# Linear attention and a top-2 mixture of experts in one kernel: the gates of both token groups in one pass behind the second list, the loads of the attention tiles and of the last weight parts moved, small work moved out of the attention loop

## The chip, the cores and the metric

The kernel runs on one core of a Trainium2 chip. The metric is the device time of one run in microseconds (us), taken as the median of several runs.

## The reference

Everything is float32. First comes a linear attention with decay, for 4 batches, 8 heads, 768 steps and a head width of 48. Its output, 3072 tokens of 384 numbers, goes into a mixture of 8 experts of which each token takes two.

```python
for t in range(S):                       # S = 768, per batch and head
    cur = einsum('bhd,bhe->bhde', u[None] * kt, vt)
    y[:, :, t] = einsum('bhd,bhde->bhe', rt, state + cur)
    state = w[None, :, :, None] * state + einsum('bhd,bhe->bhde', kt, vt)
x = y.transpose(0, 2, 1, 3).reshape(3072, 384)
logits = x @ w_gate
noisy = logits + log1p(exp(x @ w_noise)) * noise
top2 = argpartition(-noisy, 2, axis=1)[:, :2]
top2_l = take(noisy, top2) - max
top2_w = exp(top2_l); top2_w /= top2_w.sum(-1) + 1e-9
for e in range(8):                       # w1[e]: 384 x 1024, w2[e]: 1024 x 384
    out[mask] += top2_w[mask] * (maximum(x[mask] @ w1[e], 0) @ w2[e])
```

## The kernel before

**The attention loop** runs over 24 tiles of 128 tokens, `for i in range(NT)`, six chunks of each of four batches. The states of tile `i` come from chunk to chunk, so a batch's next chunk follows four tiles later. For a tile, GpSimd makes the decayed keys `kd` (`prep_k`, L402, two tiles ahead of use) and the product for the `u` term `rku` (L410 and L414, or L421 late in the loop). TensorE turns them (L225), forms the scores `PAB` (L476), the state products `RV` (L494) and the output `py` (L531). VectorE scales `rT` (L464), masks the scores into `am` (L484), updates the state (`z`, L504 and L507), reduces the `u` term to `c` (L444, in `uterm_b`), multiplies `cv` (L448, up to tile 8; later ScalarE does it), and writes the tile's tokens `x` (`xout`, L560). From tile 13 on (`PE8`) TensorE forms `c` with a product (L433), and `uterm_b` copies it (L442). `x` is turned and multiplied by both gate matrices for the logits.

**SyncE's queue** carries the loads of `k` and `r` (`load(i + 5, (0, 2))`), `v` (`load(i + 4, (2, 3))`), the noise (`load_nz`, in tiles 5 to 8), the stores of `x` into the DRAM buffer `xd`, and the parts of expert 0's weights. It works through them in the order in which they are written.

**Expert 0's weights** are loaded and split into high and low halves inside the loop, in seven parts: `W_LD` maps the tile to the part that is loaded at its end, `W_AT0` holds the tile from which a part is split. Parts 0 to 2 are w1 (`w0h`, `w0l`), parts 3 to 6 are w2 (`w1h`, `w1l`). ScalarE writes the high halves, VectorE the low halves of the parts 0 to 3 (L356 and L359, 128x512 or 128x384), GpSimd those of parts 4 to 6 (`W_POOL = 4`).

**Routing** is done in two groups of 12 tiles. `route(g)` is a generator of small VectorE steps that other work calls for (`rstep`, `steps`), with a few TensorE products: softplus, top 2, ranks by prefix sums, then for each list `drop`, which places token numbers with products by TensorE (`place`, L709). `route(0)` runs in tiles 13 to 23. Its last part, `gates`, is an exponential in 12 small steps on 128x12 (L591 to L605), then L842 to L847, then the gate columns `gd` (L851, L854), which SyncE stores beside the tokens in `xd`. At tile 22 the first list is ready: `rows` writes its token numbers (L883 to L885), and `xgather` fetches the first three token tiles with indirect DMAs of GpSimd (L1020).

```python
        while i == I_EARLY and not early_done:      # I_EARLY = 22
            rstep(1)
            maybe_early()
        if i == I_EARLY and (0, 0) not in XG:
            xgather(0, 0, 0)
```

**The experts** follow, 8 experts of two chunks each: `p1` (products `ph`, L1131), the relu on ScalarE and VectorE (L1135, L1137), and `p2` (products `pym`, L1167). The first `p1` starts right behind the last tile; `zero_out` clears the output meanwhile. `route(1)`, the second list (`list_0`), group 1's gates and their gathers (`gates_0`, `ggather`), the full lists (`rest`) and `list_1` run beside the first three chunks. Behind chunk `s == 2`, `tile_counts` (L987 to L1003) sets the counts by which later tiles are skipped. A flag that the decay `w` lies outside its allowed range is computed in the attention loop (`next(flag)` at tiles 4 and 6: L321 to L323 on VectorE, L326 on TensorE, L327 and L328 on VectorE); it and the counts decide whether a slow path runs at the end.

## Time and profile before

| | |
|---|---|
| median of 3 runs | 589.64 us (589.39 to 593.2) |
| profiled execution, its own time | 589.92 us |
| its span in the trace | 588.2 us |
| TensorE busy | 568.2 us, 97% |
| VectorE, ScalarE, GpSimd busy | 348.1, 284.5, 280.0 us |

The profiled execution took 1.7 us more than its span, since the run's time includes the start and the end around it. TensorE is busy for most of the span, so the share of busy time says little; what is of interest is the first quarter, where the attention loop, the handover to the experts and the routing lie.

### The profile page before, as it was taken

To read this page: it belongs to the slowest core of one execution; us is meant where nothing else is said; L and a number is where in the kernel's file an instruction comes from. 1 tells how busy PE (TensorE), PEld (TensorE's weight loads), DVE (VectorE), ACT (ScalarE), POOL (GpSimd) and SP (SyncE) were. 2 spreads that over 40 slices of the span, in tenths; PEclk is the share of its full clock that TensorE was granted. 3 is DMA by queue.
4 is the path that set the end of the run, shared out by engine and by line. 5 is a ranking of instruction groups with operands and counts; after the bars stand their busy time and mean duration, and the time that the engine had idled before them with its cause. 6 is when DMAs were issued, how large, how long until landed. Compare 5 with 4: busy or idle time off the path is not lost.

```text
span 588.2 us, 13907 instructions
## 1 busy us (share of the span) xinstructions
PE 568.2 (97%) x5383; PEld 543.4 (92%) x5384; DVE 348.1 (59%) x788; ACT 284.5 (48%) x712; POOL 280.0 (48%) x416
## 2 busy tenths in 40 slices
PE   8899899989999999999999999999999999999995
PEld 5799888879989999999999999999999999999995
DVE  7998698888864544556454554546363546454331
ACT  4348766842363624455445444454454455445220
POOL 8999455740336443436345453434262436423222
PEclk9999999989999999999999999999999999999999
DMA  8999889258405644765655646365845546424211
GB/s 166 224 219 205 201 202 210 83 142 258 125 35 189 184 131 120 189 138 175 108 154 164 177 116 200 98 184 127 173 118 153 169 127 187 124 82 85 67 35 42
DMA packets 143225, 86.53 MB, mean 147 GB/s; under 512 B 118624, under 2 KB 133215, under 8 KB 143152
## 3 DMA queue, kind: packets, MB, share of 16 engines
q1 hardware_dynamic: 132368, 56.76, 40.3%
q0 software_dynamic: 10160, 28.81, 16.0%
q8 instruction: 44, 0.72, 0.5%
q14 instruction: 29, 0.24, 0.1%
q10 hardware_dynamic: 624, 0.00, 0.1%
HBM read 58.81 MB, written 19.86 MB: 134 GB/s over the span
## 4 chain that ended last, share of the span: by engine, by line
PE 89%; DVE 5%; POOL 2%; issue 2%; ACT 1%; DMA 1%; POOLq 0%; ACTq 0%
PE ph L1131 37%; PE pym L1167 34%; PE py L531 4%; PE PAB L476 3%; PE pym L1160 2%; PE pym L1158 2%; PE KX L225 2%; PE py L569 1%; DVE am L484 1%; PE RV L494 1%; POOL kd L402 1%; PE RV L225 1%; PE RV L182 1%; PE RT L709 1%; PE ptm L1049 1%
## 5 line engine op out<-in xcount | busy, mean ns | idle before, releaser
L1167 PE MATMUL pym<-w1h,hb 128*128 128x384 f32 x768 | 200.3, 337 | 0.0
L1137 DVE SCALAR_TENSOR_TENSOR hb<-ph,hb 128x384 fp32r<-128x384 f32 x128 | 71.1, 556 | 116.7 <-ACT ht L1135 74.2
L1167 PEld LDWEIGHTS pym<-w1h,hb 128*128 128x128 f32 x768 | 139.3, 188 | 0.2
L1131 PE MATMUL ph<-xh,w0h 128*128 128x384 f32 (+1 forms) x384 | 136.0, 354 | 0.0
L1131 PE MATMUL ph<-xh,w0l 128*128 128x384 f32 (+1 forms) x384 | 135.6, 353 | 0.0
L1131 PE MATMUL ph<-xl,w0h 128*128 128x384 f32 (+1 forms) x384 | 130.4, 353 | 0.0
L1167 PE MATMUL pym<-w1l,hb 128*128 128x384 f32 x384 | 129.2, 336 | 0.0
L1135 ACT ACTIVATE hb<-ph 128x384 fp32r<-128x384 f32 x128 | 62.9, 492 | 106.7 <-PE ph L1131 106.7
L1192 POOL DMA_INDIRECT out_dram<-ot,TK x56 | 60.1, 1073 | 97.2 <-DVE ot L1186 42.1
L1020 POOL DMA_INDIRECT xg<-xd,GR x56 | 62.0, 1107 | 49.2 <-DVE r_e L603 24.4
L1131 PEld LDWEIGHTS ph<-xh,w0h 128*128 128x128 f32 x384 | 72.6, 189 | 3.5
L1131 PEld LDWEIGHTS ph<-xh,w0l 128*128 128x128 f32 x384 | 72.6, 189 | 3.1
L1131 PEld LDWEIGHTS ph<-xl,w0h 128*128 128x128 f32 x384 | 72.5, 189 | 3.2
L1035 POOL DMA_INDIRECT pv<-out_dram,GA x49 | 50.3, 1026 | 52.4 <-DMA out_dram<-ot,TK 39.7
L1167 PEld LDWEIGHTS pym<-w1l,hb 128*128 128x128 f32 x384 | 72.1, 188 | 0.1
L1105 ACT ACTIVATE xh<-xj 128x384 fp32r<-128x384 f32 (+1 forms) x42 | 21.1, 502 | 43.3 <-DVE xj L1103 43.1
L1175 ACT ACTIVATE ot<-pym 128x384 f32<-128x384 f32 x42 | 20.4, 486 | 39.9 <-PE pym L1167 33.1
L1106 DVE TENSOR_TENSOR xl<-xj,xh 128x384 fp32r<-128x384 f32 (+1 forms) x42 | 22.5, 535 | 24.8 <-ACT xh L1105 24.8
L1091 ACT ACTIVATE pl<-xg 128x768 uint16<-128x768 uint16 (+1 forms) x42 | 35.3, 841 | 1.4 <-DMA xd<-pl 1.4
L484 DVE TENSOR_TENSOR am<-PAB,mneg 128x512 int32<-128x512 int32 x48 | 30.8, 682 | 4.9 <-PE PAB L476 4.5
L476 PE MATMUL PAB<-rT,kT 64*128 64x128 f32 x384 | 27.7, 280 | 3.6 <-issue 3.2
L453 ACT ACTIVATE cv<-vt,c 128x48 f32<-128x48 f32 x120 | 30.2, 324 | 0.2
(276 smaller groups left out, 826.8 us busy)
## 6 DMA issues: line engine op xcount, KB each, us to landing
stg<-in_moe_w_dram SPq DMA_DIRECT2D x24, 512.0 KB, 4.7
stg<-in_moe_w_dram SPq DMA_DIRECT2D x32, 384.0 KB, 3.7
xd<-x SPq DMA_DIRECT2D x24, 196.0 KB, 3.3
rd<-in_r_dram SPq DMA_DIRECT2D x24, 192.0 KB, 4.3
vt<-in_v_dram SPq DMA_DIRECT2D x24, 192.0 KB, 4.3
out_dram<-ot SPq DMA_DIRECT2D x16, 288.0 KB, 4.1
kt<-in_k_dram SPq DMA_DIRECT2D x23, 192.0 KB, 3.8
xg<-xd,GR POOLq DMA_INDIRECT x56, 3.2
```

Source lines behind the costliest of these rows:

```text
L453: nc.scalar.activation(CV[i][:, h, :], vt[i][:, h, :], AF.Copy, scale=C8[i][:, h, :])
L476: nc.tensor.matmul(pa[:, s, p, :], kT[i][s * 64:(s + 1) * 64, p, :], rT[i][s * 64:(s + 1) * 64, p, :], start=True, stop=True)
L484: nc.vector.tensor_tensor(am[:, :, h].bitcast(I32), pa[:, :, h].bitcast(I32), mneg[:, None].to_broadcast([128, 2, NP // 2, 128]), op=ALU.b ...
L531: nc.tensor.matmul(o[qs], lhsT[:, qs], rhs, start=first[q], stop=last, skip_group_check=True)
L1020: nc.gpsimd.indirect_dma_start(out=xg[:n, :XW if e else DM], out_offset=None, in_=xd[:rows_of(early_)], in_offset=bass.IndirectOffsetOnAxi ...
L1035: nc.gpsimd.indirect_dma_start(out=pv[:n], out_offset=None, in_=out, in_offset=bass.IndirectOffsetOnAxis(ap=GA[:n, e * NJ + t:e * NJ + t + ...
L1091: nc.scalar.activation(pl[:n], XG[e, t][:n, :DM].bitcast(U16).rearrange("p (d two) -> p two d", two=2), AF.Copy)
L1131: nc.tensor.matmul(ph[:, :w_], a[:, d, fs], x[:, d, :w_], start=(j == 0), stop=(j == len(q) - 1))
L1135: nc.scalar.activation(h_[:, f, 0, :], ph[:, a:b], AF.Relu)
L1137: nc.vector.scalar_tensor_tensor(h_[:, f, 1, :], ph[:, a:b], 0.0, h_[:, f, 0, :].bitcast(F32), op0=ALU.max, op1=ALU.subtract)
L1167: nc.tensor.matmul(py, hb[:, f, a, hs], x[:, f, :], start=(j == 0), stop=(j == len(q) - 1))
L1192: st = nc.gpsimd.indirect_dma_start(out=out, out_offset=bass.IndirectOffsetOnAxis(ap=TK[:n, q:q + 1], axis=0), in_=ot[:n], in_offset=None, ...
```

## The change

It moves work, and removes little of it.

- **Loads.** From tile 8 on, `k` and `r` are loaded four tiles ahead and `v` three, in place of five and four; tile 8 itself loads nothing.
- **Weights.** Parts 4, 5 and 6 are loaded at tiles 15, 18 and 19 (before: 14, 16, 18) and split from tiles 18, 20 and 21 (before: 17, 19, 21). The low halves of parts 5 and 6 are VectorE's now.
- **Gates.** Both groups' gates are one pass, 24 wide, behind the second list. Group 0's exponential and gate store leave the loop; `route(1)` takes the first steps of group 0's full list (`rest_pre`) in their place.
- **First list.** `maybe_early` is called right behind `xout`, and the first token tile is fetched before GpSimd's `rku` of tile 23, the other two behind it.
- **Small work.** The two constants `ltri` and `ie_n` go to ScalarE at tile 5, the third into the slow path; the flag goes behind chunk `s == 2`; `uterm_b(i + 1)` runs behind `mask(i + 1)` in tiles 1 to 7 (it ran before `xout(i)`); a memset of GpSimd goes from tile 4 to tile 10; group 1's first `drop` places its products one step later (`lag` 3).

```diff
-W_LD = {3: 0, 5: 1, 7: 2, 9: 3, 14: 4, 16: 5, 18: 6}
-W_AT0 = (6, 8, 10, 12, 17, 19, 21)
-W_POOL = 4
+W_LD = {3: 0, 5: 1, 7: 2, 9: 3, 15: 4, 18: 5, 19: 6}
+W_AT0 = (6, 8, 10, 12, 18, 20, 21)
+AHEAD = (5, 4)
+I_FAR = 8
+W_POOL = (4,)
...
     def consts_v():
-        nc.vector.tensor_scalar(ltri, idif, 0.0, None, op0=ALU.is_gt)
-        nc.vector.tensor_copy(ieu, ie)
-        nc.vector.tensor_scalar(ie_n[:, 0, :], ie, float(LS), None, op0=ALU.mult)
+        nc.scalar.activation(ltri, mneg[:, 0, :], AF.Copy, scale=-1.0)
+        nc.scalar.activation(ie_n[:, 0, :], ie, AF.Copy, scale=float(LS))
...
-                              nc.gpsimd if len(units) >= W_POOL else nc.vector))
+                              nc.gpsimd if len(units) in W_POOL else nc.vector))
...
+    def rest_pre(g):
         i0, i1 = GROUPS[g]
         yield from slots(g)
         yield 0.2
-        for c in pairs(g, SLI[:, :, i0:i1], SL[g], "d"):
+        for PRE[g] in pairs(g, SLI[:, :, i0:i1], SL[g], "d"):
             yield 0.2
...
+    def gates(gs, lists=True):
+
+        i0, i1 = GROUPS[gs[0]][0], GROUPS[gs[-1]][1]
+        e2 = rtp[0].tile([128, NT], F32, name="r_e2", bufs=1)[:, :i1 - i0]
+        dn = GTS[:, 1, i0:i1]
+        yield from expneg(dn, [128, i1 - i0], "r2", e2)
+        nc.vector.tensor_scalar(dn, e2, 1.0, 1e-9, op0=ALU.add, op1=ALU.add)
+        yield
+        nc.vector.reciprocal(GTS[:, 0, i0:i1], dn)
+        yield
+        nc.vector.tensor_mul(dn, e2, GTS[:, 0, i0:i1])
+        yield
+        for g in gs if lists else ():
...
+            nc.sync.dma_start(xd[i0 * 128:i1 * 128, DM:].rearrange("(n p) e -> p n e", p=128), gd)
+            yield 0.25
...
         for _ in range(3):
-            next(ex, None)
+            next(behind, None)
+            next(behind, None)
             yield
...
-            yield from drop(g, *c, IJ_0, NJ, 0, g == 0)
+            yield from drop(g, *c, IJ_0, NJ, 0, g == 0, 3 if g else 2)
         routed.add(g)
-        if lists and not g:
-            while not early_done:
-                yield "wait"
-            for c in GATES[0]:
-                yield c
...
-        if early_done and (0, 0) not in XG:
-            xgather(0, 0, 0)
-        if i + 5 < NT:
-            load(i + 5, (0, 2))
-        if i in (4, 6):
-            next(flag)
+        if early_done and (0, 2) not in XG:
+            xgather(0, 0, 0, [t for t in chunks(0)[0] if (0, t) not in XG])
+        if i + AHEAD[i >= I_FAR] < NT and i != I_FAR:
+            load(i + AHEAD[i >= I_FAR], (0, 2))
...
-        if i == B:
+        if i == 10:
             consts_b()
...
-        if i + 4 < NT:
-            load(i + 4, (2, 3))
+        if i + AHEAD[i >= I_FAR] - 1 < NT and i != I_FAR:
+            load(i + AHEAD[i >= I_FAR] - 1, (2, 3))
...
-        if i and i + 1 < NT:
+        if CV_DVE <= i < NT - 1:
             uterm_b(i + 1)
         steps(1)
         xout(i)
...
-        if i == I_EARLY and (0, 0) not in XG:
-            xgather(0, 0, 0)
+        maybe_early()
+        if early_done and (0, 0) not in XG:
+            xgather(0, 0, 0, chunks(0)[0][:1 if i < I_EARLY else 3])
...
-                steps(3)
...
             mask(i + 1)
-            if not i:
+            if i < CV_DVE:
                 uterm_b(i + 1)
             steps(3)
             maybe_early()
-        if not i:
+        if i == 5:
             consts_v()
...
-            yield from GATES[1]
+            yield from gates((0, 1))
...
         if s == 2:
+            for _ in flag:
+                pass
             tile_counts(CAP)
```

The line numbers of the changed kernel are one higher than those of the kernel before for most of what follows. On **SyncE's queue around tile 8** before (`stg` is a weight part, `nz` the noise, `kt`, `rd` and `vt` the loads of k, r and v, of the tiles 13, 13, 12, 14, 14 and 13 in this order; the two `xd` stores are of the tiles 8 and 9):

```order
L348 DMA stg<-in_moe_w_dram 128x1024
L157 DMA kt<-in_k_dram 128x8x48
L157 DMA rd_103<-in_r_dram 128x8x48
L174 DMA nz<-in_moe_noise_dram 128x6x8
L157 DMA vt<-in_v_dram 128x8x48
L562 DMA xd<-x_146 128x392
L157 DMA kt<-in_k_dram 128x8x48
L157 DMA rd_104<-in_r_dram 128x8x48
L157 DMA vt<-in_v_dram 128x8x48
L562 DMA xd<-x_147 128x392
L348 DMA stg<-in_moe_w_dram 128x2x384
```

and the same place in the changed kernel, where the loads are of the tiles 13, 13, 12 and, in the last row, 14:

```order
L349 DMA stg<-in_moe_w_dram 128x1024
L176 DMA nz<-in_moe_noise_dram 128x6x8
L563 DMA xd<-x_146 128x392
L159 DMA kt<-in_k_dram 128x8x48
L159 DMA rd_103<-in_r_dram 128x8x48
L159 DMA vt<-in_v_dram 128x8x48
L563 DMA xd<-x_147 128x392
L349 DMA stg<-in_moe_w_dram 128x2x384
L159 DMA kt<-in_k_dram 128x8x48
```

The `xd` store of tile 8 and the noise stand ahead of the loads of tile 13 now; the store of tile 9 and the weight part stand ahead of the `k` load of tile 14.

On **VectorE from the end of tile 21 to the `x` of tile 23** (the last row of each) before; the twelve rows begin behind the list rows L883 to L885, which stand behind the `am` of tile 22 there, and the first `x` is of tile 22:

```order
L600 TENSOR_SCALAR r_e_2139<-r2r 128x12
L442 COPY c_2869<-py 128x8
L603 SCALAR_TENSOR_TENSOR r_e_2139<-r_e_2139,r2r 128x12
L560 TENSOR_TENSOR x_148<-py,cv 128x384
L603 SCALAR_TENSOR_TENSOR r_e_2139<-r_e_2139,r2r 128x12 x2
L484 TENSOR_TENSOR am<-PAB,mneg 128x2x256 x2
L603 SCALAR_TENSOR_TENSOR r_e_2139<-r_e_2139,r2r 128x12 x2
L605 SCALAR_TENSOR_TENSOR r_e_2139<-r_e_2139,r2s 128x12
L842 TENSOR_SCALAR GTS<-r_e_2139 128x12
L845 RECIPROCAL GTS<-GTS 128x12
L847 TENSOR_TENSOR GTS<-r_e_2139,GTS 128x12
L560 TENSOR_TENSOR x_149<-py,cv 128x384
```

and in the changed kernel, where the rows begin with those of the list, and `rT` and the first `am` are of tiles 23 and 22:

```order
L884 SCALAR_TENSOR_TENSOR lt<-L 128x3
L885 TENSOR_SCALAR lt<-lt 128x3
L886 TENSOR_SCALAR GR<-lt 128x3
L465 TENSOR_TENSOR rT<-RV,pwr 128x2x4x64
L485 TENSOR_TENSOR am<-PAB,mneg 128x2x256 x2
L357 TENSOR_TENSOR w1l_1322<-stg,w1h_1321 128x384
L443 COPY c_2848<-py 128x8
L561 TENSOR_TENSOR x_148<-py,cv 128x384
L485 TENSOR_TENSOR am<-PAB,mneg 128x2x256 x2
L360 TENSOR_TENSOR w1l_1322<-stg,w1h_1321 128x384
L357 TENSOR_TENSOR w1l_1322<-stg,w1h_1321 128x384
L561 TENSOR_TENSOR x_149<-py,cv 128x384
```

The list's three rows come ahead of `rT` of tile 23, the rows of the gates (L600 to L847) are gone from ahead of the last `x`, and three low halves `w1l` stand there in their place; a fourth follows behind it.

On **GpSimd at the same place** before (the `rku` of tile 23 is the second row):

```order
L359 TENSOR_TENSOR w1l_1337<-stg,w1h_1336 128x384
L421 TENSOR_TENSOR rku<-rT,kT 128x256 x2
L1020 DMA xg<-xd,GR 128x384 x3
L356 TENSOR_TENSOR w1l_1337<-stg,w1h_1336 128x384
L359 TENSOR_TENSOR w1l_1337<-stg,w1h_1336 128x384
L1020 DMA xg<-xd,GR 128x384 x3
L1020 DMA xg<-xd,GR 64x384
```

and in the changed kernel:

```order
L360 TENSOR_TENSOR w1l_1322<-stg,w1h_1321 128x384
L422 TENSOR_TENSOR rku<-rT,kT 128x256 x2
L403 TENSOR_TENSOR kd_101<-kt,tabk 128x4x48 x2
L1021 DMA xg<-xd,GR 128x384
L422 TENSOR_TENSOR rku<-rT,kT 128x256 x2
L1021 DMA xg<-xd,GR 128x384 x5
L1021 DMA xg<-xd,GR 64x384
```

The first indirect DMA stands ahead of the `rku` of tile 23, and four low halves (two of them ahead of these rows) are no longer GpSimd's but VectorE's.

## Rows read from the trace of the kernel before

**Rows 1.** Windows of 20 us: length, busy time per engine, granted clock, DMA share, GB/s

```profile
40.00:60.00 20.00, 20.00 (x546) 19.45 (x542) 17.95 (x34) 16.02 (x50) 19.12 (x33) 1.00 0.93 207
60.00:80.00 20.00, 16.75 (x438) 16.04 (x435) 15.27 (x39) 14.98 (x52) 9.68 (x16) 1.00 0.84 192
80.00:100.00 20.00, 18.42 (x496) 17.54 (x494) 17.22 (x50) 13.86 (x48) 11.83 (x21) 1.00 0.92 211
100.00:120.00 20.00, 19.27 (x505) 18.23 (x501) 16.13 (x40) 16.13 (x57) 14.61 (x21) 1.00 0.37 98
120.00:140.00 20.00, 17.33 (x176) 16.37 (x173) 17.29 (x54) 7.41 (x23) 4.46 (x5) 0.91 0.75 218
...
180.00:200.00 20.00, 20.00 (x119) 19.58 (x118) 8.30 (x13) 7.57 (x17) 12.85 (x17) 1.00 0.63 188
```

**Rows 2.** Waits of TensorE: waiter, releaser, us in total, times, longest

```profile
PE PAB L476 <- issue: 3.2, 3, 1.4
```

**Rows 3.** TensorE's timeline: start, us, what, count, idle before and its releaser

```profile
68.15 0.60 PE L476 MATMUL PAB<-rT,kT 64*128 64x128 f32 x7 [1.42 <-issue]
```

**Rows 4.** SyncE's timeline around tile 13's loads and the first stall

```profile
50.87 0.41 SPq L157 DMA_DIRECT2D kt<-in_k_dram  x1
...
51.95 2.25 SPq L174 DMA_DIRECT2D nz<-in_moe_noise_dram  x1
...
55.59 0.70 SPq L562 DMA_DIRECT2D xd<-x  x1
...
65.09 2.87 SPq L157 DMA_DIRECT2D rd<-in_r_dram  x1
```

**Rows 5.** DMA issues of the page: KB each, median us from issue to landing

```profile
kt<-in_k_dram SPq DMA_DIRECT2D x23, 192.0 KB, 3.8
```

**Rows 6.** VectorE's timeline in tiles 1 and 4, and of tile 11's x

```profile
15.98 0.61 DVE L310 TENSOR_SCALAR ltri<-stg 128x128 bf16<-128x128 int32 x1
...
17.00 0.16 DVE L312 TENSOR_SCALAR ie_n<-ie 128x8 f32<-128x8 f32 x1
...
29.11 0.54 DVE L321 TENSOR_SCALAR ok<-wp 128x4 f32<-128x4 f32 x1
...
30.22 0.16 DVE L323 TENSOR_REDUCE okb<-ok 128x1 bf16<-128x4 f32 x1
...
61.20 0.56 DVE L560 TENSOR_TENSOR x<-py,cv 128x384 f32<-128x384 f32 x1 [0.53 <-ACT cv L453]
```

**Rows 7.** GpSimd's timeline around the keys of tile 13

```profile
55.31 1.41 POOL L402 TENSOR_TENSOR kd<-kt,tabk 128x192 f32<-128x192 f32 x2
```

**Rows 8.** The whole timeline from tile 22 to the experts

```profile
117.29 1.43 POOL L421 TENSOR_TENSOR rku<-rT,kT 128x256 f32<-128x256 f32 x2 [1.23 <-DVE rT L464]
...
119.43 1.15 POOL L1020 DMA_INDIRECT xg<-xd,GR  x1 [0.71 <-DVE r_e L600]
...
122.41 2.72 DVE L603 SCALAR_TENSOR_TENSOR r_e<-r_e,r2r 128x12 f32<-128x12 f32 x2
...
122.62 1.09 PE L531 MATMUL py<-vt,am 128*64 128x48 f32 x32
123.12 1.02 POOL L356 TENSOR_TENSOR w1l<-stg,w1h 128x384 fp32r<-128x384 f32 x1
...
124.08 1.01 POOL L359 TENSOR_TENSOR w1l<-stg,w1h 128x384 fp32r<-128x384 f32 x1
...
125.94 0.56 DVE L560 TENSOR_TENSOR x<-py,cv 128x384 f32<-128x384 f32 x1
```

**Rows 9.** One line's low halves on VectorE: ns min/median/max

```profile
L356 DVE TENSOR_TENSOR w1l<-stg,w1h x1: 547/547/547, 76.9 to 76.9; 128x384 fp32r<-128x384 f32 x1
```

**Rows 10.** Window of the first expert products, columns as in rows 1

```profile
128.40:132.00 3.60, 3.60 (x16) 3.59 (x13) 2.30 (x11) 0.47 (x2) 0.00 (x0) 0.53 0.96 249
```

**Rows 11.** Timelines of VectorE and TensorE at the end of chunk 2

```profile
217.68 1.14 DVE L1186 SCALAR_TENSOR_TENSOR ot<-ot,GT,pv 128x384 f32<-128x384 f32 x2
...
220.00 0.18 PE L987 MATMUL RT<-acc,ones_b 128*128 128x8 bf16 x1
```

More of the change, by code (lines that the diff above doesn't have):

```diff
@@ L584, in T @@
         def T(nm, dt=F32):
-            t = rtp[0].tile([128, GB * (E if len(shape) == 3 else 1)], dt, name=tg + nm, bufs=1)
+            t = rtp[0].tile([128, GB * E if len(shape) == 3 else NT], dt, name=tg + nm, bufs=1)
             if len(shape) == 2:
@@ L667, in pairs, with drop @@
         yield mm2, ej2
-    def drop(g, mm2, ej2, ijv, w_, c0, first):
+    def drop(g, mm2, ej2, ijv, w_, c0, first, lag=2):
         i0, i1 = GROUPS[g]
@@ L698, in drop @@
             yield 0.05
-        late_mm.append([2, lambda: place(n, parts, pL),
+        late_mm.append([lag, lambda: place(n, parts, pL),
                         lambda: [nc.scalar.activation(ob[:, :, 1], ob[:, :, 1], AF.Copy, scale=pcol) for _, ob in parts],
@@ L717, in placed @@
             nc.vector.tensor_add(Lv, Lv, pL[:, :, :w_])
-    def rest(g):
+    PRE = {}
+    def rest_pre(g):
         i0, i1 = GROUPS[g]
@@ L722, in rest @@
         yield 0.2
-        for c in pairs(g, SLI[:, :, i0:i1], SL[g], "d"):
+        for PRE[g] in pairs(g, SLI[:, :, i0:i1], SL[g], "d"):
             yield 0.2
-        mm2, ej2 = c
+    def rest(g):
+        if g not in PRE:
+            yield from rest_pre(g)
+        mm2, ej2 = PRE[g]
         for kk in range(2):
             yield from drop(g, mm2[:, kk], ej2[:, kk], IJ_REST, (E - 1) * NJ, NJ, g == 0 and kk == 0)
-    GATES, list0 = {}, []
+    list0 = []
+    def gates(gs, lists=True):
[10 more added lines that the diff above has]
+        for g in gs if lists else ():
+            i0, i1 = GROUPS[g]
+            n = i1 - i0
+            T = T_of(n)
+            og = T("os", [128, 2, n, E])
+            nc.vector.tensor_mul(og, OHS[g], GTS[:, :, i0:i1, None].to_broadcast([128, 2, n, E]))
+            yield 0.3
+            gd = T("a")
+            nc.vector.tensor_add(gd, og[:, 0], og[:, 1])
+            while not list0:
+                yield "wait"
+            nc.sync.dma_start(xd[i0 * 128:i1 * 128, DM:].rearrange("(n p) e -> p n e", p=128), gd)
+            yield 0.25
     def route(g, lists=True, behind=iter(())):
@@ L751, in route @@
                 nc.vector.tensor_add(zp, P(0, sh), gt)
-            next(behind, None)
             yield
@@ L768, in route @@
             nc.vector.scalar_tensor_tensor(q, q, cc, s2, op0=ALU.add, op1=ALU.mult)
-            next(behind, None)
             yield
@@ L773, in route @@
         nc.vector.tensor_add(nl, q, zp)
-        for _ in behind:
-            yield
         yield
@@ L836, in route @@
         if not lists:
-            yield from slots(g, ex)
-        def gates():
-            for _ in ex:
-                yield
-            dn = GTS[:, 1, i0:i1]
-            nc.vector.tensor_scalar(dn, e2, 1.0, 1e-9, op0=ALU.add, op1=ALU.add)
-            yield
-            gts = GTS[:, :, i0:i1]
-            nc.vector.reciprocal(gts[:, 0], dn)
-            yield
-            nc.vector.tensor_mul(gts[:, 1], e2, gts[:, 0])
-            yield
-            if lists:
-                og = T("os", [128, 2, n, E])
-                nc.vector.tensor_mul(og, oh, gts[:, :, :, None].to_broadcast([128, 2, n, E]))
-                yield 0.3
-                gd = T("a")
-                nc.vector.tensor_add(gd, og[:, 0], og[:, 1])
-                while g and not list0:
-                    yield "wait"
-                nc.sync.dma_start(xd[i0 * 128:i1 * 128, DM:].rearrange("(n p) e -> p n e", p=128), gd)
-                yield 0.25
-        GATES[g] = gates()
-        if not lists:
-            yield from GATES[g]
+            yield from slots(g)
+            for _ in gates((g,), False):
+                pass
         if lists:
@@ L891, in tokens @@
         f0 = const.tile([128, E * NJ], F32, name="f0")
-        f1 = const.tile([128, E * NJ], F32, name="f1")
+        f1 = const.tile([128, E * NJ], F32, name="lt", bufs=2)
         nc.vector.tensor_scalar(ti[:, :w_], L[:, 0, a:b], -1.0, 0.0, op0=ALU.add, op1=ALU.max)
@@ L1014, in rows_of, with xgather @@
         return GROUPS[g][1] * 128
-    def xgather(e, ci, early_=-1):
-        for t in chunks(e)[ci]:
+    def xgather(e, ci, early_=-1, ts=None):
+        for t in ts or chunks(e)[ci]:
             n = tw(t)
@@ L1302, in route_when_done @@
                     at_pe[0] = 2
-                route_q.append(route(g))
+                route_q.append(route(g, True, rest_pre(0) if g else iter(())))
     def zero_out(j):
@@ L1567 @@
         if s == 2:
+            for _ in flag:
+                pass
             tile_counts(CAP)
@@ L1596 @@
             nc.vector.memset(ie_n[:, 0, 0:1], 0.0)
+            nc.vector.tensor_copy(ieu, ie)
             for i in range(NT):
```

4 lines of the change are left out of this document (1 added, 3 removed).

## Prediction, written before the changed kernel ran

> **What bounds the kernel now.** I read the windows of 20 us first. From 180 us on TensorE is busy 20.00 of 20.00 us [rows 1]: the experts are bound by their products, and the change leaves these alone. What can be won lies ahead of that. In 40 to 60 us TensorE is full too, with GpSimd at 19.12 and VectorE at 17.95: three engines at once near their limit, so that a tile there gets shorter only if all three do. In 60 to 80, 80 to 100, 100 to 120 and 120 to 140 us TensorE is idle 3.25, 1.58, 0.73 and 2.67 us, together 8.2. That, and a stretch at a lower clock (below), is nearly all that the change can give back.
>
> Then the waits and the timeline. The scores' products stop three times for 3.2 us in all with no releaser that the profile shows ("issue") [rows 2]. The longest ends at 68.15 [rows 3]. On SyncE an ordinary load's issue lasts from 65.09 to 67.96 just then [rows 4], where most issues take half a us. The two things stop together and go on together, with the DMA engines at a share of 0.84 and 0.92 in these two windows; where the share is 0.37 (100 to 120 us), TensorE loses only 0.73 us. I take the stalls to come from the crowded DMA engines, TensorE's instructions being fetched late, which the rows suggest and don't prove.
>
> Last, the handover. The products of the last tile's `py` end at 122.62 + 1.09 = 123.71, but the `x` that reads them begins only at 125.94 [rows 8]. Ahead of it in VectorE's order stand the gates' steps, and two of them took 2.72 us together, with GpSimd's low halves running from 123.12 to 125.09 beside them. TensorE stands meanwhile.
>
> **The change part by part.**
>
> *Early tiles.* The constants leave VectorE's tile 1 (15.98 to 17.16, 1.18 us) and the flag leaves tile 4 (29.11 to 30.38, 1.27 us) [rows 6]; `c` and `cv` behind the mask cost the same, but no longer stand ahead of `x`. The memset that GpSimd moves from tile 4 to tile 10 is small. So tiles 1 to 7 may come up to 2.45 us earlier. I count this at nothing, since the next load takes it back. The keys of tile 13 are multiplied at 55.31 [rows 7], 4.44 us after their load was issued at 50.87 [rows 4], and a load of that kind takes 3.8 us [rows 5]. Now the noise and the store of tile 8 stand ahead of it: 2.25 and 0.70 us of issue as they were, or some 1.2 if the noise's issue is as quick as the others. So it is issued between 52.1 and 54.0, lands between 55.9 and 57.8, and GpSimd, in order, starts tile 13's keys 0.6 to 2.5 us later than before, whatever was gained ahead. Behind them in its order stands the `rku` of tile 12, which VectorE reduces ahead of the `x` of tile 11 (61.20 [rows 6], where 0.53 us of idle time is some cover). I take +0.5, from -0.2 to +2.0: nearer the low end, because the early gain lets the other engines be done and wait.
>
> *Later loads.* The `k` of tile 14 now stands behind one more store (196 KB) and a weight part (384 KB): 0.58 MB at 192 to 207 GB/s [rows 1], 2.8 to 3.0 us. GpSimd is busy only 9.68 of 20 us from 60 on [rows 1], since its `rku` there reads `rT` and waits for it (such a wait of 1.23 us is in [rows 8]), so the keys are wanted later and this is covered. If it isn't, it is the slower rival.
>
> *The stalls.* The loads of one tile and a weight part move behind stores that wait for nothing now; SyncE's queue, which runs late there, comes nearer to the work, and TensorE has a pause ahead of the first stall in which it uses no instructions. I let the first stall (1.42) go and half of the other idle time of 60 to 100 us, (4.83 - 1.42) / 2 = 1.7. Together -3.1; the bounds are 0 (the queue is as full as before, only in another order) and -4.8 (all).
>
> *The last weight parts.* Four low halves at 0.55 us [rows 9] are 2.2 us more for VectorE in tiles 20 to 23, for four of about 1.02 on GpSimd [rows 8]. VectorE is idle 3.87 us in 100 to 120 [rows 1] and loses group 0's exponential there. Only the one beside `rku` of tile 23 can matter (next).
>
> *The handover.* Without the gates, `x` of tile 23 waits for `py` alone: at best 125.94 - 123.71 = 2.2 us. Against it, the list's rows now stand ahead of `rT` of tile 23 (three small steps like the 0.16 us one of [rows 6], with the gaps between them some 0.6 us), and GpSimd's first indirect DMA, 1.15 us, ahead of its `rku` [rows 8], which began at 117.29 as soon as `rT` was there. The DMA overlaps `rT`, so `rku` begins some 1.0 later, and `py` of tile 23 and its `x` with it, at about 124.7. The two low halves now ahead of that `x`, 1.1 us, stand in the time in which VectorE waits for `py`. I take -1.2, from -2.2 to 0.
>
> What the 2.72 us show is that a VectorE step with operands in SBUF stands still beside a GpSimd one. The Trainium skill says so as well ("SBUF — State Buffer", "Who interferes with whom": a VectorE instruction with two SBUF inputs and a GpSimd instruction that reads SBUF contend for one port pair, and the second to issue is fully blocked); the trace agrees. The rule speaks against the change in one place: a low half on VectorE has two such inputs, and one of them now meets `rku` of tile 23. By it this term would be about -0.7, the sum half a us higher.
>
> *The clock.* From 128.4 to 132 us, the first expert products ran at a granted clock of 0.53 [rows 10], so mostly at 1.2 GHz; 3.60 us would be 1.9 at 2.4 GHz, 1.7 us less. TensorE had stood before that for most of the wait for `x`. The wait shortens but doesn't go, since turning `x` and the logits still come between. I take 0, from -1.7 to 0.
>
> *The flag.* VectorE's last step ahead of it ends at 217.68 + 1.14 = 218.82; the three steps take 1.27 [rows 6], so to 220.1; TensorE comes there at 220.00 [rows 11]. Then one product, two small steps of VectorE, and only then `tile_counts`' product, which writes the same bank, and the next chunk behind it. That is a round trip that TensorE waits for: I estimate +0.5, from +0.2 to +1.2 (the whole 1.27, if VectorE is late).
>
> *Routing of group 1, the 24-wide gates.* A step of 24 columns costs about what one of 12 does, and one exponential goes away; its place is beside full products. The six steps of `rest_pre` come ahead of the first `drop` of group 1, and its products one step later. 0, within 0.5.
>
> **The sum**, against the profiled execution: 589.92 + 0.5 - 3.1 - 1.2 + 0.5 = 586.6. The median of the runs is 0.28 under the profiled one, so 586.3. 1%, 5.9 us, is about what a measurement of this kernel can tell from no change.
>
> **The rivals.**
>
> *More goes than I count.* All stalls of 60 to 100 (-4.8), the handover's -2.0 and the clock's -1.7, with +0.3 for tile 13 and +0.5 for the flag: 589.64 - 7.7 = 581.9. For it speaks that TensorE's stalls and SyncE's coincide and that the change takes traffic from there; against it, that VectorE's routing steps fill the tiles behind and that three engines are near the limit. It decides whether TensorE is busy over 19.5 of 20 us in both windows. Chance 0.25.
>
> *The stalls stay.* They come at the same products whatever the loads do, and what is won early is lost at tile 13: +0.5 - 1.2 + 0.5 = -0.2, so 589.4. The Trainium skill would have it so ("Runtime: NRT & Kernel Launch", "Instruction fetch mechanics": the sequencer fetches its next block by itself while it works on the last, and the cost is mostly hidden); by that rule the waits would not be the fetch, and no run here shows which yet. Chance 0.17.
>
> *The loads come late.* If the queue stays as late as at tile 8, the keys of tiles 13, 14 and 15 each hold GpSimd by the 2.5 us that tile 13's upper bound gives, and TensorE with it: 7.5 - 3.1 - 1.2 + 0.5 = +3.7, so 593.3. It decides from the point at which a load lands after GpSimd has finished what stands ahead of the keys, in more than one tile. For it speaks that tile 13 has only 4.44 us from issue to use already; against it, GpSimd's 10 us of idle time from 60 on. Chance 0.07, over half of it beyond +1%.
>
> **How the numbers follow.** My forecast of 586.3 (583.8 to 588.8) has a chance of 0.51. The range that holds 8 in 10 runs from the rival with more gain to a little beyond the unchanged one: 580.8 to 590.3. Faster by over 1% (under 583.7): the first rival's 0.25, and a little of the forecast's edge, 0.28. Slower by over 1%: 0.04. The rest is 0.68.
>
> **What would show it.** On the changed profile: the tiles' `x` up to tile 7 about 2 us earlier, but the one of tile 11 near 61; GpSimd waiting for a DMA at tile 13's keys; TensorE busy 18 to 19 us in both of the windows 60 to 80 and 80 to 100, with fewer "issue" waits; the last `x` directly behind the end of its `py`; a wait of half a us at the flag's product near 215 us. I am wrong if tile 11 keeps the early gain, if waits for DMA at the keys go on behind tile 13, or if the "issue" waits are as long as before.

## The result, and the profile after

The changed kernel took 596.76 us (median of 6 runs, 593.45 to 601.62), the kernel before 590.66 us beside it (6 runs, 589.39 to 593.24). The ratio is 1.010, with a 95% interval of 1.005 to 1.015. I had forecast 586.3, faster. The profiled execution is the longest of the six, 601.62 us, with a span of 599.8, and two more profiles of the same kernel (below) have spans of 596.5 and 597.0. The kernel before has two profiles as well, and both are of quick executions: 589.92 us, 0.7 under the median above, and 589.99 us on a chip on which its median was 592.5. So a difference between profiles can be larger than the one between medians.

The windows of the changed kernel, with the columns of [rows 1]:

```profile
60.00:80.00 20.00, 17.78 (x432) 17.03 (x428) 13.72 (x33) 13.86 (x48) 13.45 (x21) 0.91 0.92 212
80.00:100.00 20.00, 16.86 (x370) 16.09 (x368) 15.62 (x46) 11.25 (x39) 9.38 (x15) 0.83 0.71 155
...
120.00:140.00 20.00, 18.71 (x307) 17.49 (x303) 15.36 (x45) 11.37 (x39) 5.22 (x6) 1.00 0.57 175
...
160.00:180.00 20.00, 15.45 (x78) 13.45 (x77) 10.21 (x34) 7.71 (x16) 6.92 (x7) 0.74 0.30 84
```

Two places stand out. From 80 to 100 us TensorE is busy less than before at a granted clock of 0.83 (1.00 in the other two profiles). From 160 to 180 us it is busy 15.45 of 20 us at 0.74, where it had hardly a gap in the kernel before:

```profile
160.00:180.00 20.00, 19.77 (x120) 17.92 (x120) 14.57 (x49) 11.28 (x28) 9.00 (x12) 1.00 0.23 81
```

Three of TensorE's waits over the whole span of the changed kernel (waiter, releaser, us, times, longest); the first two lie in this second place, the last is the flag's, at 231 us:

```profile
...
PE RT L710 <- DVE r_ob L693: 3.2, 1, 3.2
...
PE RT L710 <- DVE r_sl L646: 1.0, 1, 1.0
...
PE RT L988 <- DVE bad L328: 0.2, 1, 0.2
```

The first row is a placement of token numbers that waits for VectorE. The VectorE timeline shows what VectorE did instead:

```profile
158.07 0.25 DVE L758 TENSOR_TENSOR r_a<-r_os 128x96 f32<-128x96 f32 x1
...
158.97 0.30 DVE L693 TENSOR_TENSOR r_ob<-r_de,ij 128x300 bf16<-128x300 bf16 x1
162.90 0.26 DVE L758 TENSOR_TENSOR r_a<-r_os 128x96 f32<-128x96 f32 x1 [3.62 <-DMA xd<-r_a]
163.08 0.31 DVE L696 TENSOR_TENSOR r_ob<-r_ob,thi 128x300 bf16<-128x300 bf16 x1
```

and SyncE's and TensorE's timelines the two sides of it:

```profile
160.26 3.31 SPq L761 DMA_DIRECT2D xd<-r_a  x2
...
164.07 0.43 PE L710 MATMUL RT<-r_ob,r_oa 128*128 128x100 bf16 x6 [3.17 <-DVE r_ob L693]
165.45 0.66 PE L710 MATMUL RT<-r_ob,r_oa 128*128 128x100 bf16 x6 [0.95 <-DVE r_sl L646]
...
172.14 1.32 PE L1132 MATMUL ph<-xl,w0h 128*128 128x448 f32 x3
```

`gates((0, 1))` makes the gate columns of both groups in one pass and in one buffer, `gd = T("a")`, the trace's `r_a`. Group 0's columns are ready at 158.3; their store is issued at 160.26. Group 1's columns go into the same buffer, so VectorE stands until the first store has read it, 3.62 us, and `r_ob`, which the placement needs, stands behind that in VectorE's order. TensorE loses 3.17 and 0.95 us, and goes on at half its clock: three products there take 1.32 us, and the two windows of 4 us from 164 to 172 us were granted 0.55 and 0.50. The store is late itself: it is issued 1.94 us after its columns are ready. In the kernel before, group 0's columns are ready at 127.06, their store is issued at 127.08, and the next writer of the buffer waits 0.77 us. SyncE's waits in the changed kernel name what the stores stand for, the indirect DMAs that fetch tokens out of the same DRAM buffer `xd`; the last of these ahead of the store is issued at 157.24, and such a DMA takes 2.5 to 3.2 us to land. In the kernel before, the second store stands for them in the same way (ready at 152.16, issued at 156.37, the last fetch at 153.28), but there nothing waits for the buffer:

```profile
SPq L761 <- DMA xg<-xd,GR: 14.2, 3, 11.9
```

The start of some tiles' `x`, and what of the span lies behind the last one, in profiled executions:

| kernel | tile 7 | tile 11 | tile 21 | tile 23 | behind it |
|---|---|---|---|---|---|
| before | 43.82 | 61.20 | 115.83 | 125.94 | 462.3 |
| before, second profile | 44.21 | 62.46 | 116.29 | 126.40 | 461.8 |
| changed | 42.44 | 64.05 | 121.12 | 130.00 | 469.8 |
| changed, second | 41.85 | 62.64 | 116.99 | 125.87 | 470.6 |
| changed, third | 42.00 | 64.29 | 117.83 | 126.70 | 470.3 |
| gates alone | 43.85 | 61.76 | 116.61 | 124.52 | 470.4 |
| gates alone, two buffers (fourth chip) | 45.94 | 65.42 | 118.93 | 126.83 | 462.5 |
| gates alone, two buffers (third chip) | 43.79 | 61.72 | 115.01 | 126.38 | 467.1 |
| all but the gates | 41.85 | 64.29 | 117.22 | 126.15 | 462.3 |
| all but the gates, second | 41.98 | 63.48 | 117.83 | 126.77 | 461.5 |
| all but the gates, list at its old place (third chip) | 41.75 | 65.21 | 120.25 | 131.70 | 470.9 |

The last column is the span less the start of the last `x`. It is 7.5 to 8.8 us longer in all three profiles of the changed kernel, while the loop varies by several us between executions. The column is no measure of the gates alone, as the two rows of the third chip show (more on them below).

### The profile page after: what moved, and what is told of

Its sections match the earlier page's. It is cut to its first block, busy times and chain, and to the rows that moved or that the text cites. A ratio compares the mean times of both kernels' runs of the same rounds, so it can differ in the third digit from the quotient of the medians.

```text
span 599.8 us, 13890 instructions
## 1 busy us (share of the span) xinstructions
PE 574.7 (96%) x5383; PEld 549.0 (92%) x5384; DVE 346.3 (58%) x774; ACT 284.9 (47%) x714; POOL 273.8 (46%) x412
## 4 chain that ended last, share of the span: by engine, by line
PE 82%; issue 5%; DMA 4%; POOL 3%; DVE 2%; SPq 1%; ACT 1%; POOLq 0%; DVEq 0%; ACTq 0%
PE ph L1132 35%; PE pym L1168 32%; PE py L532 4%; PE PAB L477 2%; PE pym L1159 2%; PE pym L1161 2%; DMA kt<-in_k_dram 1%; DMA rd<-in_r_dram 1%; PE KX L227 1%; SPq L159 1%; POOL kd L403 1%; PE RV L227 1%; POOL rku L411 1%; PE py L570 1%; DMA xd<-x 1%
## 5 line engine op out<-in xcount | busy, mean ns | idle before, releaser
L1193 POOL DMA_INDIRECT out_dram<-ot,TK x56 | 58.5, 1045 | 102.5 <-DVE ot L1187 48.9
L1036 POOL DMA_INDIRECT pv<-out_dram,GA x49 | 49.0, 1001 | 46.2 <-DMA out_dram<-ot,TK 32.3
L403 POOL TENSOR_TENSOR kd<-kt,tabk 128x192 f32<-128x192 f32 x46 | 28.9, 648 | 6.5 <-DMA kt<-in_k_dram 6.0
```

What stands on the lines that cost most here:

```text
L403: nc.gpsimd.tensor_mul(KD[i][:, h], kt[i][:, h], tabk[:, h, :D])
L1036: nc.gpsimd.indirect_dma_start(out=pv[:n], out_offset=None, in_=out, in_offset=bass.IndirectOffsetOnAxis(ap=GA[:n, e * NJ + t:e * NJ + t + ...
L1193: st = nc.gpsimd.indirect_dma_start(out=out, out_offset=bass.IndirectOffsetOnAxis(ap=TK[:n, q:q + 1], axis=0), in_=ot[:n], in_offset=None, ...
```

## The experiments

The runs were made on five chips, each with runs of the kernel before on the same chip. The kernel before took 591.7 to 598.2 us on them, so ratios are compared on one chip; where they aren't, it is said. An "us" between two kernels is the difference of their medians, and a ratio need not be that of the medians to the last digit.

**First chip** (kernel before 596.64 us). Two buffers, in the changed kernel:

```diff
-            gd = T("a")
+            gd = T("s" if g else "a")
```

> The changed kernel, with a second buffer for the gate columns of group 1. Theory A (one buffer): in the changed kernel VectorE stands 3.62 us at L758 because the gate columns of group 1 are written into the buffer that the store of group 0's columns still reads; TensorE then waits 3.17 and 0.95 us for the placement products and its clock falls to 0.55 and 0.50. So here the wait at L758 is gone, TensorE waits under 1.5 us between 156 and 172 us, the clock stays at 1.00 there, and the time is 4 to 8 us under the changed kernel's 596.8: 589 to 592. Rival B (the attention loop alone makes the loss, and the store's wait is only seen because the loop ended late): the time stays at 595 to 598. Rival C (the clock falls by itself from run to run): the wait goes, the clock falls anyway, 593 to 597.

594.54 us, ratio 0.9974 (0.9944 to 1.0003). The times that I expected were set from a kernel before of 590.66 us; on this chip it took 6 us more, so the 594.54, which lies in the range of rival C, decides nothing. The wait and the clock do: VectorE's wait is gone, and TensorE's row in the stretch is

```profile
156.00:176.00 20.00, 17.69 (x118) 15.61 (x117) 13.40 (x45) 10.05 (x24) 7.47 (x8) 1.00 0.34 97
```

against this one in the changed kernel:

```profile
156.00:176.00 20.00, 15.24 (x85) 13.37 (x85) 9.16 (x30) 6.24 (x15) 8.77 (x9) 0.74 0.39 108
```

and this one in the kernel before (both where the kernel before took 590.66 us):

```profile
156.00:176.00 20.00, 19.77 (x128) 17.57 (x127) 14.47 (x49) 10.98 (x28) 6.59 (x7) 1.00 0.27 83
```

The clock stays up, but 2.1 us of idle time remain over the kernel before; 1.07 of them are a later placement that waits for ScalarE, a wait that other kernels on this chip show too (below). Loads as before, in the changed kernel (`I_FAR = 99`):

> The changed kernel, with all loads of k, r and v five and four tiles ahead as before. Theory D (the nearer loads cost the loop): in the changed kernel GpSimd waits 2.0 and 2.5 us for DMAs at the keys, the loop ends 4 us later, and two stalls of TensorE behind bursts of loads pull its clock down. So here the last x begins at 123 to 126 us in place of 130.0, GpSimd's waits at the keys are under 1 us each, and the time is 591 to 594. Rival E (the early tiles' reordering or the weight parts do it): the last x stays at 129 to 131, the time at 595 to 598.

598.19 us, 1.0026 (0.9996 to 1.0056). The wait of VectorE is there (TensorE waits 3.1 us for `r_ob`). The last `x` begins at 126.26, near the 126 that theory D allowed, but the time is not the 591 to 594 that it asked for, GpSimd waits 4.8 us in all for the keys' loads here too, and the changed kernel's second profile has 125.87 without the edit: the loop of the first profile was a late one. Both edits:

> The changed kernel with both of these edits. If A and D both hold and are independent, 585 to 588, under the kernel before; if one of them stands for the other (the clock falls once in any case), 590 to 593.

593.76 us, 0.9953 (0.9926 to 0.9981). Against the run with the loads alone back it is 0.73% or 4.4 us faster: the price of the one buffer on this chip, from one line. Against two buffers alone it is 0.8 us, too little to tell. And the loads alone, in the kernel before:

```diff
-        if i + 5 < NT:
-            load(i + 5, (0, 2))
+        if i + (4 if i >= 8 else 5) < NT and i != 8:
+            load(i + (4 if i >= 8 else 5), (0, 2))
```

and the same for `v`.

> The kernel before with the nearer loads alone (four and three tiles ahead from tile 8, no load at tile 8). Theory D: the last x is 1 to 5 us later than in the kernel before (125.9), the time 591 to 595. Rival E: the last x within 1 us, the time 589 to 591. My prediction's account (less traffic ahead of the stalls) would make it 586 to 588.

596.03 us, 1.0007 (0.9981 to 1.0033): nothing that can be measured. GpSimd waits 2.9 us for the keys of tile 13, as the prediction had it, and whatever the loads cost or give lies within 0.4% either way. Theory D falls, and so does the gain that I expected of the loads.

**Second chip** (kernel before 592.5 us). The changed kernel again:

> The changed kernel as it is, for a second profile and beside the others of this call on one chip. Theory A (the second gate columns wait in the one buffer): the wait at L758 is again 3 to 4 us and TensorE again stands about 4 us between 156 and 172 us of the span; time 0.3 to 1.0% over the kernel before. Rival C (the loss in the first profile was a bad execution): no such wait, time within 0.3%.

598.55 us, 1.0101 (1.0067 to 1.0136); VectorE's wait is 3.69 us. The gates' edits alone, on the kernel before:

```diff
-            yield from GATES[1]
+            yield from gates((0, 1))
...
-                route_q.append(route(g))
+                route_q.append(route(g, True, rest_pre(0) if g else iter(())))
```

with the new functions that they need.

> The kernel before with the gates of both groups in one pass behind the second list and the first steps of group 0's full list in route(1), and nothing else of the change. Theory A: the same wait of VectorE for the first store, 3 to 4 us, and 0.4 to 1.0% slower than the kernel before; the last x of the loop earlier by 1 to 2 us, since no gate step stands ahead of it. Rival F (the loss needs the other parts, which bring the experts and the gate stores closer together): no wait at L758 over 1 us, time within 0.3% or faster.

595.51 us, 1.006 (1.0027 to 1.0094). The wait is 3.5 us, the last `x` at 124.52 is the earliest of all profiles, and the 470.4 us behind it are those of the changed kernel. Rival F falls. But the changed kernel is 3.0 us slower still on the same chip, by the medians. All but the gates:

> The change without its gates: loads, weight parts, constants, flag, the order of c and cv, the first list early, but each group's gates where the kernel before has them. Theory A: no loss, time within 0.4% of the kernel before on either side. Rival E (the loop's edits cost most): 0.5 to 1.0% slower.

589.21 us, 0.9938 (0.9914 to 0.9961). So the rest of the change makes the kernel faster, by 3.3 us (3.7 by the ratio), more than the 0.4% that I had allowed, and the gates turn it round. The kernel before, for its profile:

> The kernel before as it is, for a profile on the chip of this call, as the base of the others. Both theories: no wait for a gate store over 1 us; span within 1% of 588.2.

589.99 us, span 588.2. The clock falls at the first expert products again (0.91 in 120 to 140 us), and no gate store is waited for over 0.4 us. GpSimd waits 2.10 us for the keys of tile 13 here too, which it didn't in the first profile of the kernel before.

**Third chip** (kernel before 598.17 us). The gates alone, with two buffers:

> The gates part alone on the kernel before, with a second buffer for group 1's gate columns. Theory A: VectorE's wait for the first store is gone, the clock stays at 1.00 between 140 and 180 us, and against the gates part with one buffer (1.006 of the kernel before) the time falls by 0.4 to 0.8%, to 0.998 to 1.002; what stays is some 2 us of TensorE waiting for placements, which the earlier last x (1.9 us) pays for. Rival G (not the wait, but the 24-wide steps ahead of the placements make the loss): it stays at 1.004 to 1.007.

594.05 us, 0.9925 (0.9889 to 0.9962): faster than I expected of it. VectorE's wait is gone, but the clock doesn't stay at 1.00 as theory A asked: a later placement waits 2.65 us for ScalarE at 174.74, and the clock falls to 0.53 behind it. TensorE's idle time filled, in the changed kernel, ahead of the second placement of group 0's full list (`fill` is 52 there and 0 elsewhere):

```diff
+        pf = pL.rearrange("p a b -> p (a b)")
+        for _ in range(fill):
+            nc.tensor.matmul(pf, ones_b, im.rearrange("p a b -> p (a b)")[:, :pf.shape[1]], start=True, stop=True, skip_group_check=True)
```

> The changed kernel with 52 extra products of 100 columns on TensorE ahead of the placement that waits for VectorE; they write into the PSUM columns that this placement overwrites, so they change nothing but TensorE's idle time, some 3 us. Theory H (most of the loss is the clock that falls behind the wait): the wait itself stays for VectorE, but the clock stays at 1.00 behind it, and the time falls from 1.010 of the kernel before to 1.003 to 1.006. Rival (the wait itself is the loss, and the clock falls or not without weight): 1.009 to 1.012.

597.71 us, 0.9997 (0.9964 to 1.003), outside both ranges; the changed kernel did not run on this chip, so it was repeated (below). The small work and the early list alone, with the gates, loads and weights of before:

> The kernel before with the small work moved, the flag and the first list early, but its own gates, loads and weight parts. Theory I (the gain of the change without its gates, 0.6%, comes from the handover and the early tiles): 0.991 to 0.996. Rival J (it comes from less DMA traffic ahead of the stalls, by the loads and weight parts): 0.998 to 1.002.

597.21 us, 0.9985 (0.9953 to 1.0017). It falls in the range of rival J, but doesn't show it: the change without its gates did not run on this chip. All but the gates, and the list at its old place:

> The change without its gates, and with the first list where the kernel before has it (behind the mask of tile 22, its three token tiles fetched behind rku of tile 23). Theory K (the early list gives the handover something): 0.2 to 0.4% slower than with the early list (0.994), so 0.996 to 0.998. Rival L (what the early fetch wins at the last x it loses at tile 23's rku): the same, 0.992 to 0.996.

598.97 us, 0.9999 (0.9971 to 1.0028), outside both ranges. Inconclusive for the same reason, and for another: on the first, third and fifth chip, where the kernel before took 596 to 598 us, all profiles but one (the loads back, first chip) show a wait of a placement for ScalarE between 170 and 182 us that isn't there on the others, with the old gates (2.28 us with the small work and the list alone, 3.28 with the loads alone, 3.70 here) and with the new ones (2.65 with the gates alone and two buffers, about 1 us elsewhere). The kernel before has no profile on these chips, and why the wait is there stays open.

**Fourth chip** (kernel before 591.69 us). The four kernels that had to stand side by side:

> The changed kernel again, as the base of the three others on one chip. By both earlier measurements 1.010 of the kernel before; on a chip on which the kernel before is slow itself (over 595 us) 1.003 to 1.008.

596.93 us, 1.0073 (1.0045 to 1.0101).

> The changed kernel with TensorE's idle time filled with 52 products that change nothing. Theory H (the clock's fall is most of the loss): 0.4 to 0.8% faster than the changed kernel on this chip, with the clock at 1.00 behind the wait in the profile and VectorE's wait still 2.5 us or more. Rival: within 0.2% of it.

595.69 us, 1.0087 (1.0044 to 1.0131): not told apart from the changed kernel, 1.2 us under it by the medians and above it by the ratio. With five runs, that neither shows the gain of 0.4 to 0.8% that I expected nor rules its lower end out. In the profile the fill does what it should: VectorE still waits 3.5 us, but the clock stays at 1.00,

```profile
156.00:176.00 20.00, 17.67 (x156) 15.66 (x155) 12.25 (x40) 9.67 (x22) 6.67 (x7) 1.00 0.31 85
```

and the time behind the last `x` is 466.2 us, against 470.3 in the changed kernel on this chip, 4.1 less. The two profiled executions are the fastest of the five and the slowest of the six. What the timed runs lost elsewhere I can't say.

> The gates part alone with two buffers. Theory A: at least 0.8% faster than the changed kernel on this chip, and within 0.4% of the kernel before or faster. Rival G (the 24-wide steps are the loss): within 0.4% of the changed kernel.

590.45 us, 0.9958 (0.9928 to 0.9988): 6.5 us under the changed kernel on the same chip, for one buffer and the parts left out. Its row,

```profile
156.00:176.00 20.00, 18.77 (x124) 16.68 (x123) 14.46 (x53) 11.32 (x27) 7.77 (x8) 1.00 0.32 90
```

keeps 1.0 us of the idle time.

> The change without its gates. By the earlier measurement 0.994 of the kernel before; if that was the chip's doing, 0.998 to 1.001.

589.49 us, 0.9968 (0.9926 to 1.001): 7.4 us under the changed kernel. The ratio lies between the two that I had named, and its interval holds both.

**Fifth chip** (kernel before 597.93 us). The gates alone with two buffers, their steps behind the placements:

```diff
-        ga = gates_0()
-        for _ in range(6):
-            yield next(ga)
         for c in rest(0):
             yield c
-            next(ga, None)
-        for c in ga:
+        for c in gates_0():
             yield c
```

> The gates part alone with two buffers, and all its steps behind the placements of group 0's full list (they stood between its first ones). Theory G2 (the steps delay the placements): TensorE's waits for placements between 155 and 165 us fall under 0.3 us, and the time is 0.992 to 0.996 of the kernel before, at least 0.1% under the one with the steps between. Rival M (the gathers of the gates then come too late for the first outputs): 0.997 to 1.003.

599.94 us, 1.0017 (0.9987 to 1.0048), in rival M's range, though the trace shows another cause than M's (the kernel with the steps between did not run on this chip): the waits between 155 and 165 us are down to 0.32 and 0.42 us, but the later lists come later, and a placement then waits 3.63 us for VectorE:

```profile
179.85 0.43 PE L709 MATMUL RT<-r_ob,r_oa 128*128 128x100 bf16 x6 [3.63 <-DVE r_ob L692]
```

And the changed kernel with two buffers, and loads and weight parts as before:

> The changed kernel with two buffers, and with the loads and the last weight parts as before: the gates, the early list, the small work and the flag. If these add up, 0.991 to 0.995; if the handover is won only once (the early list gives what the missing gates give), 0.995 to 0.998.

595.05 us, 0.9957 (0.9931 to 0.9984). That is in the range of a handover that is won only once, though the interval reaches into the other one. The handovers themselves (from the `x` of tile 21 to that of tile 23) speak for it: on the second and fourth chip they take 7.91 and 7.90 us with the gates alone, 8.93 and 8.94 with all but the gates, 8.88 and 8.87 with both, against 10.11 in the kernel before.

## Why the prediction was wrong

**The step that failed** is the last of the sum: "Routing of group 1, the 24-wide gates. A step of 24 columns costs about what one of 12 does, and one exponential goes away; its place is beside full products. ... 0, within 0.5." The steps do cost what I said (0.17 to 0.18 us each), but I priced the arithmetic and not the two stores at its end. Leaving the gates out of the change gives back 9.3 us on the second chip (598.55 less 589.21) and 7.4 on the fourth, where I had 0. In the kernel before, each group's columns had a store of its own some 30 us apart; in the change they stand one behind the other in one buffer, on the engine on whose next steps TensorE's placements wait. That a moved step's DMAs count, and that whoever writes a buffer waits for the DMA that reads it, could have been read from the diff and the order of instructions. That it is this wait is shown: one line that gives the second store its own buffer takes the wait away, and with it 4.4 us (first chip). On the fourth chip two buffers, with the other parts left out as well, are 6.5 us faster. In the profiled executions the time behind the last `x` grows by 7.5 to 8.8 us: by one pair of profiles, 4.1 us of it is the clock, and some 4.1 the two waits (3.17 + 0.95), of which 0.55 to 0.58 us stay with two buffers. That the clock costs as much in the timed runs is not shown. Of VectorE's 3.62 us, 1.94 are the late issue of the first store. No run changes the fetches that SyncE waits for, so what an earlier store would give is not measured.

The parts don't add up. On the second chip the gates alone cost 3.0 us, the rest alone gains 3.3, and both together cost 6.05, not -0.3. Some 2.2 us of that gap are the handover, which either part shortens and both together shorten no further; the rest of it stays open.

**Early tiles and tile 13.** Right in what was seen, not shown in its cause. Tile 7's `x` is 1.4 to 2.4 us earlier and the gain is gone at tile 11. In two of the three profiles GpSimd waits for a load at the keys of tiles 11 and 13; the first two rows below are of the changed kernel, the third is tile 13 in the second profile of the kernel before:

```profile
48.38 1.15 POOL L403 TENSOR_TENSOR kd<-kt,tabk 128x192 f32<-128x192 f32 x2 [2.52 <-DMA kt<-in_k_dram]
...
59.29 1.60 POOL L403 TENSOR_TENSOR kd<-kt,tabk 128x192 f32<-128x192 f32 x2 [2.04 <-DMA kt<-in_k_dram]
...
57.65 1.14 POOL L402 TENSOR_TENSOR kd<-kt,tabk 128x192 f32<-128x192 f32 x2 [2.10 <-DMA kt<-in_k_dram]
```

I took +0.5 (to +2.0) at tile 11; against both profiles of before it was between +0.2 and +3.1. The keys of tile 13 begin at 57.88 to 59.62 in the three profiles, all behind the 57.8 that I had as the latest. The base was one execution: at 57.65 the kernel before waits for the same load, with the old distance, so the runs don't show that the later issue made the wait. And a load is waited for two tiles earlier already, at 48.38, ahead of anything that the new distance touches: with the early tiles faster, the loads of before are late as well.

**The stalls**, -3.1 in the sum, are the second term that failed: they didn't go. From tile 11 to tile 21 the changed kernel's second and third profiles take 54.35 and 53.54 us, the kernel before 54.63 and 53.83: no difference beyond that between executions. In the first profile it is 57.07, with two stalls, the longer of them this one,

```profile
93.53 0.59 PE L227 MATMUL RV<-ident,rd 64*128 64x64 f32 x7 [2.15 <-issue]
```

behind which the clock was down to 0.56 in the window from 96 to 100 us. The "issue" waits sum to 3.7, 3.2 and 2.0 us in the three profiles, against 3.7 and 3.5 in the two of before. TensorE is busy 16.86 to 17.78 us in both of the windows 60 to 80 and 80 to 100, not the 18 to 19 that I gave as a sign, and in all three profiles the window 60 to 80 was granted 0.91, against 1.00 twice before. The waits move to other products; the loads' new order doesn't end them. The rival "the stalls stay" had this right. But what it rested on, that the fetch of instructions is hidden, the traces speak against. In the first profile of before the four waits of over 0.3 us end at 68.15, 73.81, 79.34 and 95.45, and 16 KB transfers on the queue of instructions (q8) start at 65.71, 71.45, 76.97 and 93.06, each 2.4 us ahead. All 17 such waits from 60 to 105 us in these five profiles end 2.2 to 3.0 us behind the start of one, while such a transfer starts only every 5 us or so. So my account of the stalls, instructions that come late, fits; that the loads' order decides it does not.

**The handover**, -1.2, was right to the tenth in its number: tiles 22 and 23 take 10.11 us before (125.94 - 115.83) and 8.88, 8.88 and 8.87 in the three profiles of the changed kernel. In detail the list and its DMA ahead of `rku` delay tile 22 (5.34 us against 4.45), and tile 23 takes 3.54 in place of 5.66, its `x` close behind `py`, whose products end at 129.90:

```profile
130.00 0.56 DVE L561 TENSOR_TENSOR x<-py,cv 128x384 f32<-128x384 f32 x1 [0.31 <-ACT cv L454]
```

The cause is not the one I gave: all but the gates, with the gates' steps left in the loop, takes 8.93 and 8.94, so the rest of the change wins this, and taking the gates out as well adds 0.05 us. The gates alone take 7.91 and 7.90, the 2.2 us that I had as the best case; the rest of the change takes 1.0 us of that back, the size that I had estimated for the early list. Which of its parts do either, no run separates on these chips. Where the low half and `rku` meet, they take 0.93 and 1.74 us in place of 0.55 [rows 9] and 1.43 [rows 8]. This is the contention that the Trainium skill describes ("SBUF — State Buffer", "Who interferes with whom"); the trace agrees. The half us that my estimate added for it doesn't show in the term, which came out at -1.2:

```profile
123.86 0.93 DVE L357 TENSOR_TENSOR w1l<-stg,w1h 128x384 fp32r<-128x384 f32 x1
...
123.63 1.74 POOL L422 TENSOR_TENSOR rku<-rT,kT 128x256 f32<-128x256 f32 x2
```

**The clock** at the first expert products, which I left as it was, stayed at 1.00 in all three profiles of the changed kernel (120 to 140 us; 0.91 in [rows 1]). It does so without the gates too, but the time behind the last `x` is 462.3 and 461.5 us there, and 462.3 and 461.8 in the kernel before, so the 1.7 us that I had as a bound are not seen.

**The flag** made TensorE wait 0.2 us (L988 above); I had taken 0.5.

**The sum.** Without the gates' term I had -3.3 us. The change without its gates measured -3.3 us (0.9938) and -2.2 (0.9968). That the size agrees is luck: most of mine was the stalls, which didn't go. Where the gain comes from is not shown. The two profiles have spans of 588.4 and 588.3 us, the two of the kernel before 588.2, so these executions have no gain to look for.

**The best version** of those run is the change without its gates (0.9938 and 0.9968), or the gates alone with two buffers (0.9925 and 0.9958); each is faster than both kernels, though one interval of the first reaches 1.001, and the runs don't tell the two apart. The changed kernel with two buffers and the loads as before (0.9953, first chip), and with the weight parts as before too (0.9957, fifth), lie in the same range.

## What to carry to other kernels

When steps are merged and moved, follow each of their stores to the buffer that it reads: two stores from one buffer, one behind the other, make the in-order engine that fills it wait until the first is issued and has read it, and everything queued behind waits too. Look also at what the store itself waits for in its new place. Merge such steps only with a buffer for each store, and look at who waits for the engine's next instructions in the new place. A change of many parts is best priced, and run, with each part left out once: here the gates alone were worth +0.6%, the rest -0.6%, and both together +1.0%, so the parts alone would not have told it either.

## What the runs showed of the hardware

In eight profiles the granted clock fell from 1.00 to 0.50 or little over it, which is 1.2 GHz of 2.4, behind a wait of 2.65 to 3.70 us on TensorE. It was back at 1.00 after 10 to 12 us in four of them (the changed kernel three times, the gates alone), which were 7.5 to 8.8 us longer behind the last `x` than the kernel before, about twice the wait. It was back within 4 to 6 us in the other four; in one of these, the changed kernel with the loads back, the waits are the same 3.14 and 0.96 us, and the stretch is 3.6 us longer than with two buffers on the same chip. Behind a wait of 3.28 us (the loads alone, first chip) it stayed at 1.00. So the price of such a wait is not fixed; where the clock stayed low for 10 us, about half of it was the clock (4.1 us by the filled kernel's profile).

The "issue" waits of TensorE end 2.2 to 3.0 us behind the start of a 16 KB transfer of instructions, 17 of 17, in a stretch in which the DMA engines are busy at a share of 0.71 to 0.98.

The same kernel took 591.7 us on one chip and 598.2 on another, and the ratio of a changed kernel to it moved with the chip by up to 0.9 per cent (the filled kernel, 0.9997 and 1.0087), as much as the whole change is worth. The three chips on which the kernel before took over 596 us are those whose profiles show a placement waiting for ScalarE; their handovers are longer as well, 10.1 to 10.3 us in place of 8.9 with both parts of the change, and 11.4 in place of 7.9 with the gates alone and two buffers.
